# One of four exponential patterns made by an accumulating DMA, in two of three batches

## The chip, the core and the metric

The kernel runs on one core of one Trainium2 chip. The metric is device time in microseconds (us) of that core. The kernel before has a median of 757.29 us in three runs (756.96 to 757.34).

In what follows TensorE (PE in the profile) multiplies matrices, ScalarE (ACT) evaluates functions, VectorE (DVE) and GpSimd (POOL) do elementwise work, and SyncE (SP) issues most DMAs. SBUF is the on-chip memory, PSUM the accumulator memory that TensorE writes, in eight banks of 512 columns.

## The reference

Two attention blocks read the same input x (2048 tokens, 512 features, 32 heads of 16) and are mixed by a gate per token.

```python
x = A_x
g = _sigmoid((x * gate_w).sum(-1, keepdims=True))
# block A: softmax attention
qkv = (x @ wqkv).reshape(B, S, 3, H, Dh)            # q, k, v of 32 heads
scores = jnp.einsum("bhqd,bhkd->bhqk", q, k) * (Dh ** -0.5)
o = jnp.einsum("bhqk,bhkd->bhqd", softmax(scores), v)
a = o.transpose(...).reshape(B, S, D) @ wo
# block B: linear attention with a softmax feature map
phi = concat[softmax(p @ w_phi), softmax(-(p @ w_phi))]   # for q and for k
kv, z = sum_s phi_k v, sum_s phi_k
b = ((phi_q kv) / (phi_q z + 1e-6)).reshape(B, S, D) @ wo
return g * a + (1 - g) * b
```

The exponentials of block A are by far the most work: 32 heads x 2048 x 2048 scores.

## The kernel before

**Tiles.** Scores are kept transposed: keys on the partitions, queries along the columns. A tile (unit) is 128 keys by 512 queries of one head. Four heads make a pack of four tiles, in the four row strips of TensorE; 16 packs, one for each block of 128 keys, make a group of 64 tiles that sums into one PSUM bank; there are 32 groups, so 2048 tiles. A tile goes one of two ways.

**ScalarE's way** (`_qk`, L1040; `_exp`, L1088; `_pv`, L1147). TensorE writes the scores of two tiles into a ring of four PSUM banks, ScalarE takes both in one exponential of 1024 columns into `ET`, a ring of 22 tiles in SBUF (`NSLOT`), and TensorE multiplies by the values V and adds into the group's bank.

**VectorE's way** (`_vector_batch`). `NUMS` says how many tiles of each group go this way, 504 in all. They are handled in batches of four. For each tile TensorE writes scores into a spare bank, and VectorE forms from them, with one multiply and add written as a 16-bit integer (`v_bits`, L946), the bit pattern of a bf16 number that approximates the exponential. One such pattern is coarse, so four are used, with 0, 31, 64 and 95 added to the integer; TensorE multiplies the first two by V and the others by `V2`, which is V times 0.703125, and sums all four. VectorE makes the other three for a whole batch of four tiles (2048 columns) in two additions (`v_step`, L971): the first 2048 columns plus 31 gives the second pattern, then both, 4096 columns, plus 64 give the third and fourth.

```python
src, dst = (va[:, 0, 0:n], va[:, 1, 0:n]) if k == 1 else (va[:, :, 0:n], vs[:, :, 0:n])
```

**Block B and the projections.** They are woven in between: GpSimd does the masks for `qT` (L803), part of the tree sums (L1339), reciprocals (L1392 to L1398), ratio products (L1382), the scaled values V2 (L844) and the normalisation product into T (L1185). SP issues DMAs: four-way copies (T to T, L1191) and DMA transposes that bring normalised outputs (`back`, L1195), feature maps (`phit`, L1451) and block B's outputs (`ontb`, L1509) into the layout for the next product, and the stores (L1653).

**The order.** All instructions of all engines are put in order at build time by a planner (`Plan`). `op` records each operation with its cost, priority and dependences; `order` repeatedly takes, over all engines, the operation that can start earliest by the planned costs, then by priority. `port` keeps GpSimd's operations and VectorE's wide SBUF operations apart in that plan. `shift` adds a pseudo-random offset from `SEEDS` to priorities. On TensorE the planner inserts products with a block of zeros (L1154) where the engine would be little used. On the chip each engine then runs its list strictly in order and waits on semaphores (`emit`, `_waits`).

Of the kernel before, what the change touches and what calls it, by code (L numbers as in the profile page):

```python
# [39 lines left out]
class Op:  # L40
    def __init__(self, eng, fn, cost, name, prio, rel, kind, lat):
        self.eng, self.fn, self.cost, self.name = eng, fn, cost, name
        self.prio, self.rel, self.kind, self.lat = prio, rel, kind, lat
        self.deps = []
        self.users = []
        self.left = 0
        self.need = False
        self.acquire = None
        self.release = None
        self.also = None  # L50
        self.twin = None
# [11 lines left out]
        self.group = None  # L63


class Plan:
# [11 lines left out]
    def __init__(self):  # L78
        self.ops = []
        self.now = -1  # L80
        self.free_banks = []
        self.keep = None
        self.open = None
        self.pad = None
        self.mode = None
        self.strip = [0.0] * 4
        self.n_qk, self.qks, self.exps = 0, (), ()
        self.n_acc = 0
        self.half = None
        self.todo = {}  # L90

# [18 lines left out]
    def op(self, eng, fn, cost, reads=(), writes=(), deps=(), name="", prio=0.0, rel=-99, kind="full",  # L110
# [23 lines left out]
        o.port = eng == "POOL" or eng == "DVE" and name in self.PORT  # L134
# [5 lines left out]
    SEEDS = (3340, 7601, 0, 849, 2310, 7659, 5600, 4117, 3297, 4434, 5571, 2308, 3491, 696, 0, 2037, 1043, 4583, 3197, 9690, 0, 1465, 7801, 8165, 7230, 6142, 5708, 481, 3824, 4801, 1237, 3959, 2876, 7231)  # L140

    def shift(self):
        count = {}
        for o in self.ops:
            k = count[o.name] = count.get(o.name, 0) + 1
            s = self.SEEDS[min(max(int(o.prio // 16), 0), 33)] if o.prio >= 0 else 0
            if s:
                h = sum(map(ord, o.name)) * 7919 + k * 104729 + s * 65537
                h = (h ^ h >> 13) * 2654435761 & 0xFFFFFFFF
                o.prio += (s % 3 + 1) * (((h ^ h >> 16) & 1023) / 511.5 - 1)  # L150
# [64 lines left out]
    def order(self):  # L215
        avail = {e: [] for e in self.ENGS}
        for o in self.ops:
            o.left = len(o.deps)
            for d in o.deps:
                d.users.append(o)  # L220
# [9 lines left out]
        while left:  # L230
            best = None
# [94 lines left out]
    def emit(self, nc, ctx):  # L326
# [6 lines left out]
        count = dict.fromkeys(self.ENGS, 0)  # L333
        for e, q in self.queues.items():
            for o in q:
                if o.name.startswith("dma"):
                    o.sem = (ctx.enter_context(nc.semaphore(o.name)), 16 * len(o.fn) if isinstance(o.fn, list) else 16)
# [70 lines left out]
class _Kernel:  # L408
    NRING = 4
    GROUPS = (2, 2)  # L410
    NSLOT = 22
# [4 lines left out]
    NA, NST, LEAD = 2, 2, 7  # L416
# [21 lines left out]
    ALONE, EARLY = 12, 10  # L438
    PVP = 10
# [18 lines left out]
    def build(self):  # L458
        with ExitStack() as ctx:
# [10 lines left out]
            p.shift()  # L470
# [4 lines left out]
    def _memory(self, ctx):  # L475
# [67 lines left out]
        tiles = [sb(f"vs{k}", [P, 2, self.PACK, QCH], U16) for k in range(self.NST + self.NA)]  # L543
        self.vs, self.va = tiles[:self.NST], tiles[self.NST:]
# [15 lines left out]
    def dma(self, eng, name, fn, cost=0.5, writes=(), reads=(), prio=0.0, rel=-99, lat=2.2, deps=()):  # L560
        return self.plan.op(eng, fn, cost, name="dma_" + name, writes=writes, reads=reads, prio=prio, rel=rel,
                            lat=lat, deps=deps)

# [322 lines left out]
    NUMS = (6, 10, 16, 14, 14, 16, 16, 19, 13, 19, 17, 12, 17, 11, 19, 19, 14, 20, 12, 16, 19, 13, 17, 16, 15, 20, 12, 20, 17, 21, 21, 13)  # L886

    def _plan_vector(self):
# [13 lines left out]
        self.hooks = {}  # L902
# [17 lines left out]
    def _vector_batch(self, number, units, due):  # L920
# [10 lines left out]
        for j, u in enumerate(units):  # L931
# [16 lines left out]
            if j < 2 * pairs and j % 2:  # L948
# [4 lines left out]
                def two(e, j=j, jobs=twin[j // 2]):  # L953
                    lo, hi = sorted(x.bank for x in jobs)
                    return bits(e, va[:, 0, j - 1:j + 1, :], self.ps[:, lo:hi + 1:hi - lo, :])
                parts.append(op("DVE", two, self.c_dve(1024), deps=[first[0], m] + war, name="v_bits", prio=first[2],
                                release=first[1], also=job))
            else:
                parts.append(op("DVE", lambda e, j=j, job=job: bits(e, va[:, 0, j, :], self._bank(job)),
# [4 lines left out]
        slot = self.n_step % self.NST  # L964
        self.n_step += 1
        vs, b_vs, b_vb = self.vs[slot], self.b_vs[slot], self.b_vb[number % self.NA]
        for k in range(4):
            tile, buf = (vs if k > 1 else va)[:, k % 2], b_vs if k > 1 else b_vb if k else b_va
            if k in (1, 2):
                src, dst = (va[:, 0, 0:n], va[:, 1, 0:n]) if k == 1 else (va[:, :, 0:n], vs[:, :, 0:n])  # L970
                o = op("DVE", lambda e, k=k, src=src, dst=dst: e.tensor_scalar(dst, src, float(STEPS[k - 1]), None,  # L971
                                                                               op0=ALU.add),
                       0.16 + k * n * QCH * 0.00026, reads=[b_va] + [b_vb] * (k - 1), writes=[buf], name="v_step",
                       prio=units[0] / 4 - 4)
                o.urgent = units[0] // 4 - self.AHEAD + 2
            v, bufs = (self.V, self.b_V) if k < 2 else (self.V2, self.b_V2)
            for g in sorted({u // (4 * NT) for u in units}):
# [8 lines left out]
                x = op("PE", run, 0.23, reads=[buf], deps=list(found.values()), name="pvx", prio=units[0] / 4 - 2,  # L986
# [6 lines left out]
    def _attention(self):  # L993
        plan, NT, NQC = self.plan, self.NT, self.NQC
        NU = 4 * self.NPACK
        self.exps, self.qks, self.pvs = [], [], []
        self._plan_vector()
# [8 lines left out]
        self.b_va, self.b_vb = [Buf() for _ in range(self.NA)], [Buf() for _ in range(self.NA)]  # L1006
        self.b_vs = [Buf() for _ in range(self.NST)]
        self.n_step = 0
# [9 lines left out]
        self.bank2 = [0, 0]  # L1018
# [60 lines left out]
    def _exp(self, a, b, half=None):  # L1079
# [11 lines left out]
        if a >= len(self.mine) - NR:  # L1091
            o.on_commit = lambda o: plan.free_banks.extend((x % NR, plan._seen(o, "PE"), [o]) for x in range(a, b))
# [70 lines left out]
    def _norm(self, qc, src, side, last, dst, b_dst, due, job, alone=False):  # L1163
# [25 lines left out]
        if side == 1 and not alone and self.P_BACK:  # L1189
# [4 lines left out]
            self.dma("SP", f"mix{due}", parts, cost=11.0, reads=[b_T2], writes=[self.b_T3], prio=due, lat=1.5)  # L1194
            self.dma("SP", f"back{due}", lambda e: e.dma_start(dst.rearrange("p (b t) -> p b t", b=4),  # L1195
                                                               self.T3[:].rearrange("p b f -> p (b f)"), transpose=True),
                     cost=1.3, reads=[self.b_T3], writes=[b_dst], prio=due, lat=1.7)
# [251 lines left out]
    def _b_phit(self, tt, slot, k, due):  # L1449
        op = self.plan.op  # L1450
        self.dma("SP", f"phit{self.n_phit}", lambda e: e.dma_start(  # L1451
            self.phiT[:, :, tt * TOK:tt * TOK + TOK], self.bq[:, slot, k], transpose=True), cost=1.35,
            reads=[self.b_bq[slot]], writes=[self.b_phiT[tt]], prio=due, lat=2.3)
# [53 lines left out]
    def _b_ontb(self, t, due):  # L1507
        tt, slot = t % 4, t % 2
        self.dma("SP", f"ontb{t}", lambda e: e.dma_start(  # L1509
            self.onTB[:, :, tt * TOK:tt * TOK + TOK], self.onB[:, slot, :], transpose=True), cost=1.25,  # L1510
            reads=[self.b_onB[slot]], writes=[self.b_onTB[tt]], prio=due + 1, lat=1.6)
# [84 lines left out]
    def _out(self, qc):  # L1596
        op, NT, NQC = self.plan.op, self.NT, self.NQC
        for tt in range(4):
# [23 lines left out]
            if final and ring:  # L1622
                job.bank = (self.bank2[1] + tt - 4 + self.RINGOUT) % self.NRING
            for x in first:
# [28 lines left out]
            s = self.dma("ACT" if final and tt % 2 else "SP", f"out{t}", lambda e, t=t: e.dma_start(  # L1653
                self.out2d[t * TOK:(t + 1) * TOK, :], self._out_tile(t)), cost=0.36, reads=[b_outt], prio=due)
# [44 lines left out]
```

## Time and profile before

| what | value |
|---|---|
| median of three runs | 757.29 us (756.96 to 757.34) |
| profiled execution: span from first to last instruction | 755.8 us |
| profiled execution: own time beside the span | not listed apart; the runs lie 1.5 us above the span |
| busy ACT / DVE / PE / POOL | 741.1 / 719.9 / 744.3 / 228.6 us |
| ScalarE's exponentials (L1088) | 774 |
| VectorE's bit steps (L946) and additions (L971) | 504 and 252 |
| granted TensorE clock | 1.000 |

The busy times are unions of intervals. Neighbouring instructions on one engine overlap, so a mean duration is longer than the distance from one start to the next. TensorE's busy time contains products that are pipelined and the products with zeros, so it does not say that TensorE is full. The chain of the profile goes back from the last instruction through whatever released each step.

### The profile page before, as it was taken

The page shows a single profiled execution, that of the slowest core. Times are in us where ns is not written, and L with a number is a line of the kernel's source. Part 1 is how long each engine was busy: PE and PEld are TensorE (multiplying, and loading weights), DVE is VectorE, ACT ScalarE, POOL GpSimd, SP SyncE. Part 2 cuts the span into 40 slices and gives each one's busy share as a digit, 9 for nine tenths or more (in the row PEclk, how much of TensorE's full clock was granted, in tenths as well). Part 3 has the DMA queues.
Part 4 walks back from the last instruction along what each step waited for, and adds up shares of the span by engine and source line. Part 5 has one row for each costly group of instructions (what it writes and reads, how often), then busy time and mean ns, then how long its engine had stood idle before and what let it go on. Part 6 is the DMA issues. An engine that isn't in the chain of part 4 may idle for free.

```text
span 755.8 us, 17204 instructions
## 1 busy us (share of the span) xinstructions
PE 744.3 (98%) x7246; PEld 219.7 (29%) x7246; DVE 719.9 (95%) x1128; ACT 741.1 (98%) x796; POOL 228.6 (30%) x317
## 2 busy tenths in 40 slices
PE   8999999999999999999999999999999999999998
PEld 3323222323332222222232323222232222223222
DVE  4788999999999999999999999999999999999997
ACT  6999999999999999999999999999999999999996
POOL 2213206241534334234407051431615051260010
PEclk9999999999999999999999999999999999999999
DMA  9610000001001000000200312112022103111010
GB/s 220 144 24 6 9 8 6 12 2 15 2 2 15 1 8 10 6 11 3 42 15 19 40 24 48 30 34 39 8 47 33 29 23 44 22 30 28 2 15 29
DMA packets 89181, 20.79 MB, mean 28 GB/s; under 512 B 83472, under 2 KB 88592, under 8 KB 89104
## 3 DMA queue, kind: packets, MB, share of 16 engines
q1 hardware_dynamic: 87232, 18.92, 13.8%
q8 instruction: 56, 0.92, 0.5%
q10 hardware_dynamic: 1872, 0.79, 0.4%
q14 instruction: 21, 0.17, 0.1%
HBM read 4.21 MB, written 2.10 MB: 8 GB/s over the span
## 4 chain that ended last, share of the span: by engine, by line
ACT 69%; PE 18%; DVE 11%; DMA 1%; issue 0%
ACT ET L1088 67%; PE ps L1147 6%; PE ps L1040 6%; DVE vs L946 4%; PE ps L711 4%; DVE vs L971 3%; ACT bq L1335 3%; PE ps L1154 1%; DMA xT<-in_A_x_dram 1%; DVE bq L1332 1%; DVE onB L1500 1%; DVE T L1168 0%; DVE rinvB L1483 0%; DVE btree L1329 0%; DVE btree L1327 0%
## 5 line engine op out<-in xcount | busy, mean ns | idle before, releaser
L1088 ACT ACTIVATE ET<-ps 128x1024 bf16<-128x1024 f32 (+1 forms) x774 | 713.4, 1158 | 1.9 <-PE ps L1040 1.5
L946 DVE TENSOR_SCALAR vs<-ps 128x512 uint16<-128x512 f32 x504 | 323.5, 678 | 12.0 <-PE ps L1040 10.1
L1040 PE MATMUL ps<-qT,kT 32*128 32x512 bf16 (+1 forms) x2052 | 307.3, 384 | 4.1 <-ACT ET L1088 2.0
L971 DVE TENSOR_SCALAR vs<-vs 128x2048 uint16<-128x2048 uint16 (+1 forms) x252 | 241.8, 973 | 1.3 <-PE ps L1147 0.5
L1147 PE MATMUL ps<-vs,V 128*32 128x512 bf16 x2016 | 216.9, 384 | 1.1 <-DVE vs L971 0.7
L1147 PE MATMUL ps<-ET,V 128*32 128x512 bf16 x1544 | 193.8, 387 | 0.4 <-DVE vs L946 0.2
L1040 PEld LDWEIGHTS ps<-qT,kT 32*128 32x128 bf16 x2052 | 76.4, 91 | 300.4 <-ACT ET L1088 287.5
L1339 POOL TENSOR_TENSOR btree<-btree 128x512 f16<-128x512 f16 (+1 forms) x32 | 35.7, 1117 | 208.0 <-DVE btree L1337 207.0
L1147 PEld LDWEIGHTS ps<-ET,V 128*32 128x32 bf16 x1544 | 48.6, 94 | 81.3 <-issue 72.2
L1147 PEld LDWEIGHTS ps<-vs,V 128*32 128x32 bf16 x2016 | 50.1, 95 | 49.9 <-issue 28.0
L711 PE MATMUL ps<-WB,xT 128*128 128x512 bf16 x192 | 58.6, 384 | 0.0
L1154 PE MATMUL ps<-kT,zero 128*32 128x512 bf16 x604 | 58.4, 385 | 0.0
L1324 POOL TENSOR_SCALAR bq<-bq 128x1024 bf16<-128x1024 bf16 x16 | 20.2, 1262 | 105.8 <-DVE bq L1306 64.9
L803 POOL TENSOR_SCALAR qT<-qtmp,mask 128x512 bf16<-128x512 bf16 x30 | 26.7, 897 | 55.6 <-DVE qtmp L798 51.0
L711 PE MATMUL ps<-xT,WA 128*128 128x512 bf16 x120 | 37.1, 384 | 0.3 <-DVE onB L1500 0.3
L1185 POOL TENSOR_TENSOR T<-T,rinv 128x512 bf16<-128x512 f32 x15 | 19.6, 1305 | 55.1 <-DVE rinv L1183 54.9
L1335 ACT ACTIVATE bq<-bq 128x2048 bf16<-128x2048 bf16 x16 | 32.8, 2047 | 0.0
L1168 DVE STREAM_TRANSPOSE T<-ps 128x512 f32<-128x512 f32 x32 | 22.6, 706 | 4.5 <-PE ps L1147 4.4
L1306 DVE CAST bq<-ps 128x512 bf16<-128x512 f32 x32 | 21.6, 679 | 0.7 <-PE ps L711 0.6
L844 POOL TENSOR_SCALAR V<-V 128x544 bf16<-128x544 bf16 x16 | 10.7, 670 | 36.0 <-DVE V L837 35.7
L711 PEld LDWEIGHTS ps<-WB,xT 128*128 128x128 bf16 x192 | 13.1, 97 | 24.8 <-issue 20.5
L1332 DVE TENSOR_TENSOR bq<-bq,btree 128x2048 bf16<-128x2048 bf16 x16 | 19.8, 1240 | 0.0
(91 smaller groups left out, 420.9 us busy)
## 6 DMA issues: line engine op xcount, KB each, us to landing
T<-T SPq DMA_DIRECT2D x240, 8.0 KB, 1.8
WB<-in_B_wqkv_dram SPq DMA_DIRECT2D x1, 1536.0 KB, 8.6
out_dram<-WB SPq DMA_DIRECT2D x12, 128.0 KB, 1.7
WA<-in_A_wqkv_dram SPq DMA_DIRECT2D x2, 384.0 KB, 5.3
WoB<-in_B_wo_dram SPq DMA_DIRECT2D x1, 512.0 KB, 3.9
WoA<-in_A_wo_dram SPq DMA_DIRECT2D x1, 512.0 KB, 4.8
WA<-in_A_wqkv_dram ACTq DMA_DIRECT2D x2, 128.0 KB, 3.3
WA<-in_A_wqkv_dram ACTq DMA_DIRECT2D x1, 256.0 KB, 4.9
```

Source lines behind the costliest of these rows:

```text
L711: return e.matmul(out, lhs, rhs, start=start, stop=stop)
L803: x = self.plan.op("POOL", lambda e, side=side: e.tensor_scalar(self.qT[:, s0 + side, :], tmp, self.mask[:, side:side + 1], 0.0, op0=ALU.m ...
L946: bits = lambda e, to, src: e.tensor_scalar(to, src, SCALE * LOG2E * 128.0, float(ORIGIN), op0=ALU.mult, op1=ALU.add)
L971: o = op("DVE", lambda e, k=k, src=src, dst=dst: e.tensor_scalar(dst, src, float(STEPS[k - 1]), None, op0=ALU.add), 0.16 + k * n * QCH * 0 ...
L1040: return e.matmul(out[:, cols], self.kT[32 * i:32 * i + 32, cp, kt * TOK:(kt + 1) * TOK], self.qT[32 * i:32 * i + 32, s, cols], start=True ...
L1088: o = plan.op("ACT", lambda e: e.activation(self.ET[:, a % NS:a % NS + n, cols], self.ps[:, a % NR:a % NR + n, cols], ACT.Exp, scale=SCALE ...
L1147: ins = e.matmul(self._bank(ot)[32 * i:32 * i + 32, :], v[:, v0:v0 + 32], tile, start=(kt == 0), stop=(kt == self.NT - 1), tile_position=( ...
L1154: ins = e.matmul(self._bank(ot)[32 * i:32 * i + 32, :], self.zero[:], self.kT[:, 0, 0:QCH], start=False, stop=False, tile_position=(0, 32 ...
L1168: t1 = op("DVE", lambda e: e.transpose(T1[:, side].rearrange("p b s -> p (b s)"), src()), 0.735, deps=last, writes=[b_T1[side]], name="n_t ...
L1332: + [("b_sub", two(2048), lambda e: e.tensor_tensor(x, x, spread(tree[:, :, 0]), ALU.subtract))],
L1335: op("ACT", lambda e: e.activation(flat, flat, ACT.Exp), 1.789, reads=[b], writes=[b], name="b_exp", prio=due + 1)
L1339: + [("b_sum", two(128 * n), lambda e, n=n: e.tensor_tensor(half[:, :, 0:n], half[:, :, 0:n], half[:, :, n:2 * n], ALU.add), (n <= self.P_ ...
```

## The change

In two of three batches (`KINDS = 'DDV'`; not in the first four nor the last two, `PLAIN`) the pattern with 64 added is no longer made by VectorE. After TensorE has used the first pattern, GpSimd issues a DMA that adds a constant tile `steps`, filled with 64, to the tile in place (`accum_op=ALU.add`), and TensorE reads the same tile again as the third pattern. In the other batches VectorE makes the same addition in place. The patterns with 31 and 95 are made by VectorE from the first, each by an addition of 2048 columns, so no addition of 4096 columns is left. The buffers change with it: five tiles `va` that hold a first pattern, two pairs `vb`, the constant tile, and `ET` with 16 tiles instead of 22.

`NUMS` gives VectorE 548 tiles instead of 504 (60 instead of 46 in the first four groups). The planner now has a model of the time for which the DMA engines are moving an addition (`moves`, `chan`): copies and transposes that are issued meanwhile are planned to land later. A DMA issue on GpSimd does not count for `port`. The offsets of `shift` are drawn anew every eight steps of the plan from 64 new seeds, so that the whole order differs.

```diff
-        o.port = eng == "POOL" or eng == "DVE" and name in self.PORT
+        o.port = eng == "POOL" and not name.startswith("dma") or eng == "DVE" and name in self.PORT
...
+    EVERY = 8
+    FIRST, LANDED, BEHIND = 1.45, 1.3, 1.5
...
+                if o.moves > 0:
+                    self.chan = max(t + self.FIRST, self.chan) + o.moves
+                    o.lat = self.chan + self.LANDED - o.end
+                    for x in self.small:
+                        if x.end + x.lat > t + self.FIRST:
+                            x.lat = max(x.lat, self.chan + self.BEHIND - x.end)
+                elif o.moves <= -100:
+                    o.lat = max(o.lat, self.chan + self.BEHIND - o.end)
+                    self.small = [x for x in self.small if x.end + x.lat > t] + [o]
+                elif o.moves < 0:
+                    o.lat += min(-o.moves, max(0.0, self.chan - o.end))
...
-    NSLOT = 22
+    NSLOT = 16
...
-    NA, NST, LEAD = 2, 2, 7
+    NA, NB, LEAD = 5, 2, 7
...
+    C_ADD, MOVES, ADD_AT, PVD = 0.9, 2.8, -1, 0
+    KINDS, PLAIN = 'DDV', (4, 2)
...
-    NUMS = (6, 10, 16, 14, 14, 16, 16, 19, 13, 19, 17, 12, 17, 11, 19, 19, 14, 20, 12, 16, 19, 13, 17, 16, 15, 20, 12, 20, 17, 21, 21, 13)
+    NUMS = (8, 16, 20, 16, 16, 20, 17, 15, 18, 18, 18, 18, 15, 18, 17, 15, 18, 17, 16, 16, 18, 20, 17, 21, 16, 16, 16, 18, 16, 21, 20, 17)
...
-        for k in range(4):
-            tile, buf = (vs if k > 1 else va)[:, k % 2], b_vs if k > 1 else b_vb if k else b_va
-            if k in (1, 2):
-                src, dst = (va[:, 0, 0:n], va[:, 1, 0:n]) if k == 1 else (va[:, :, 0:n], vs[:, :, 0:n])
-                o = op("DVE", lambda e, k=k, src=src, dst=dst: e.tensor_scalar(dst, src, float(STEPS[k - 1]), None,
-                                                                               op0=ALU.add),
...
+        tiles = [(va, b_va), (vb[:, 0], b_v1), last, (va, b_va)]
+
+        def make(dst, by, reads, writes, prio):
+            o = op("DVE", lambda e: e.tensor_scalar(dst[:, 0:n], va[:, 0:n], float(by), None, op0=ALU.add),
+                   0.16 + n * QCH * 0.00026, reads=reads, writes=writes, name="v_step", prio=prio)
...
+        def add(k, tile, buf):
+            o = self.dma("POOL", f"add{number}_{k}", lambda e: e.dma_start(tile[:, 0:n], self.steps[:, 0:n], accum_op=ALU.add),
+                         cost=self.C_ADD, reads=[self.b_steps], writes=[buf], prio=units[0] / 4 + self.ADD_AT)
...
+        make(vb[:, 0], STEPS[0], [b_va], [b_v1], units[0] / 4 - 4)
+        if kind != "E":
+            make(vb[:, 1], sum(STEPS), [b_va], [b_v3], units[0] / 4 - 4)
+        for k in (0, 1, 2, 3) if kind != "E" else (0, 1, 3, 2):
+            tile, buf = tiles[k]
+            if k == 3 and kind == "V":
+                make(va, STEPS[1], [], [b_va], units[0] / 4 - 1)
+            elif k == 3 or k == 2 and kind == "E":
+                add(k, tile, buf)
```

More of the change, by code (lines that the diff above doesn't have):

```diff
@@ L216, in order @@
         avail = {e: [] for e in self.ENGS}
+        count = {}
         for o in self.ops:
+            k = count[o.name] = count.get(o.name, 0) + 1
+            o.base, o.code = o.prio, sum(map(ord, o.name)) * 7919 + k * 104729
             o.left = len(o.deps)
@@ L562, in dma, with moving @@
                             lat=lat, deps=deps)
+    def moving(self, o, moves, late=0.0):
+        o.moves = -moves
+        o.lat += late
+        return o
     def _loads(self):
```

89 lines of the change are left out of this document (53 added, 36 removed).

## The prediction

> **What bounds the kernel now.** I read the head of the page first, then its chain, then the groups by shape, the stretches of 25 us, and last the chain and the timeline piece by piece.
>
> ```profile
> span 755.8 us, 17204 instructions
> PE 744.3 (98%) x7246; PEld 219.7 (29%) x7246; DVE 719.9 (95%) x1128; ACT 741.1 (98%) x796; POOL 228.6 (30%) x317
> ACT 69%; PE 18%; DVE 11%; DMA 1%; issue 0%
> ```
>
> ScalarE is busy for 741.1 of 755.8 us and carries 69% of the chain, so its work sets the end. VectorE is close behind with 719.9. The three runs have a median of 757.29 us, 1.5 us above this span; I sum against the span and add 1.5 at the end. A difference of 0.2% (1.5 us) is about what a measurement of this kernel can tell from none.
>
> The stretches say where each engine has room (columns: PE, PEld, DVE, ACT, POOL busy):
>
> ```profile
> 0.00:25.00 25.00, 22.57 (x140) 8.79 (x143) 14.29 (x26) 17.92 (x23) 6.27 (x18) 1.00 1.05 229
> 25.00:50.00 25.00, 25.00 (x244) 8.08 (x237) 18.45 (x27) 25.00 (x29) 6.07 (x8) 1.00 0.17 47
> 50.00:75.00 25.00, 25.00 (x206) 8.17 (x204) 22.78 (x38) 25.00 (x27) 5.79 (x11) 1.00 0.10 22
> 75.00:100.00 25.00, 24.99 (x234) 6.90 (x231) 23.69 (x41) 25.00 (x29) 5.12 (x7) 1.00 0.08 12
> ...
> 550.00:575.00 25.00, 24.22 (x278) 7.78 (x277) 24.67 (x39) 25.00 (x27) 9.82 (x15) 1.00 0.17 32
> ...
> 725.00:750.00 25.00, 24.93 (x259) 7.19 (x258) 23.32 (x37) 22.42 (x25) 0.00 (x0) 1.00 0.07 10
> 750.00:775.00 25.00, 2.79 (x13) 1.07 (x11) 2.41 (x4) 1.08 (x2) 0.00 (x0) 0.98 0.06 21
> ```
>
> ScalarE's 14.7 us of idle time lie almost wholly at the start (7.1) and the end (2.6 and 4.7). VectorE's 35.9 split otherwise: 10.7, 6.6, 2.2 and 1.3 in the first 100 us (20.8), 1.7 and 3.4 in the last two rows (5.1), and so only 10.0 in the 625 us between. There both engines are nearly full, and a change pays only if it takes work from both.
>
> **What one operation costs.** A group's mean is a duration, and neighbours overlap, so I count from start to start. In the chain in order of time (start, length, what), and in the timeline of VectorE:
>
> ```profile
> 560.88 49.50 ACT ET L1088 x54
> ```
>
> ```profile
> 373.97 1.21 DVE L971 TENSOR_SCALAR vs<-vs 128x4096 uint16<-128x4096 uint16 x1
> 375.10 0.68 DVE L946 TENSOR_SCALAR vs<-ps 128x512 uint16<-128x512 f32 x1
> 375.70 0.24 DVE L1476 SCALAR_TENSOR_TENSOR rinvB<-ps,ghB,eps 128x32 f32<-128x32 f32 x1
> 375.85 0.68 DVE L971 TENSOR_SCALAR vs<-vs 128x2048 uint16<-128x2048 uint16 x1
> 376.45 0.24 DVE L1476 SCALAR_TENSOR_TENSOR rinvB<-ps,ghB,eps 128x32 f32<-128x32 f32 x1
> ```
>
> One exponential of two tiles costs ScalarE 49.50/54 = 0.917 us. On VectorE the next instruction starts 0.60 us after a 512-column bit step (375.10 to 375.70), 0.60 after a 2048-column step (375.85 to 376.45) and 1.13 after a 4096-column one (373.97 to 375.10).
>
> **ScalarE.** 548 tiles instead of 504 go to VectorE, so 44/2 = 22 exponentials fall away: 22 x 0.917 = 20.2 us. Busy 741.1 becomes 720.9; with its idle time unchanged the span is 735.6, the time 737.1. That is the floor on this engine.
>
> **VectorE.** Groups by shape of before (count, then busy and mean):
>
> ```profile
> L946 DVE TENSOR_SCALAR vs<-ps 128x512 uint16<-128x512 f32 x504 | 323.5, 678 | 12.0 <-PE ps L1040 10.1
> L971 DVE TENSOR_SCALAR vs<-vs 128x4096 uint16<-128x4096 uint16 x126 | 154.9, 1233 | 0.8 <-PE ps L1147 0.5
> L971 DVE TENSOR_SCALAR vs<-vs 128x2048 uint16<-128x2048 uint16 x126 | 89.1, 713 | 0.5
> ```
>
> In the issue order of the changed kernel stand 548 bit steps, no 4096-column step, and 324 of 2048 columns: two for each of 137 batches and a third for the 50 that VectorE completes itself. The other 87 batches have a DMA issue on POOL instead. Added: 44 x 0.60 = 26.4 and 324 x 0.60 = 194.4; removed: 126 x (0.60 + 1.13) = 218.0. The net is +2.8 us, so VectorE needs 722.7. The eleven extra batches eat what the DMA saves; the gain is ScalarE's alone, provided VectorE finds room in a shorter span: at 735.6 its idle time must fall from 35.9 to 12.9.
>
> Where is that room? One tile cost 0.60 + 1.73/4 = 1.03 us; it now costs 0.90 in a DMA batch, 1.05 in a VectorE batch, 0.95 in the two-to-one mix. The 32 groups of 64 tiles take 23.6 us each, so the first four are the first 94 us; there the table gives VectorE 60 tiles instead of 46. The first sixteen are plain: 16 x 1.05 + 44 x 0.95 - 46 x 1.03 = +11.2 us, against 10.1 idle after the first 25 us and 10.7 in them, which is mostly waiting for the loads. ScalarE would allow 7 x 0.917 = 6.4 there; I take half, 3.2. In the other 28 groups (488 tiles for 458) VectorE saves 458 x 1.03 - 488 x 0.95 = 8.1 us, and ScalarE 15 x 0.917 = 13.8. If VectorE keeps its 10.0 us of idle time, this part gains 8.1; if it gives up 5.7 of them, 13.8. I take 13.8, because the largest part of that idle is the row's 10.1 us of bit steps that wait for scores, a wait that the slower ScalarE leaves room for, not a need. So 757.3 - 3.2 - 13.8 = 740.3, between 749.2 (8.1, and nothing early) and 737.1.
>
> **The DMA and its wait.** Each of the 87 adds a constant tile to 128x2048 two-byte elements, 512 KB, in place in SBUF. No such transfer is in the trace. Nearest rows:
>
> ```profile
> T<-T SPq DMA_DIRECT2D x240, 8.0 KB, 1.8
> WoB<-in_B_wo_dram SPq DMA_DIRECT2D x1, 512.0 KB, 3.9
> WoA<-in_A_wo_dram SPq DMA_DIRECT2D x1, 512.0 KB, 4.8
> ```
>
> A plain load of the same size lands 3.9 us after its issue, against 1.8 for a small copy, so its moving takes about 2.1. An addition in place has two tiles to read; with the moving doubled I estimate 6.0 us (ends: 3.9, and 4.8 plus 3.0 = 7.8 with the slower load doubled likewise). TensorE takes its instructions in order, so when it reaches the values of this pattern too early, scores and then ScalarE stop behind it. The issue order fixes how early: between TensorE's last read of the tile as bits and its read after the addition lie 4 score pairs that wait for ScalarE in 1 batch, 5 in 3, 6 in 6, 7 in 17, 8 in 14, more in 46. At 0.917 us each that is 3.7, 4.6, 5.5, 6.4 and 7.3 us. About 0.9 us of a stall is hidden, since the four score banks hold one activation ahead. At 6.0 us the cost is (2.3 - 0.9) + 3 x (1.4 - 0.9) = 2.9 us; at 3.9 nothing. I take 2.9: 743.2, rounded to **743**.
>
> **What I cost at nothing.**
>
> ```profile
> L1147 PE MATMUL ps<-vs,V 128*32 128x512 bf16 x2016 | 216.9, 384 | 1.1 <-DVE vs L971 0.7 <-DVE vs L946 0.4
> L1154 PE MATMUL ps<-kT,zero 128*32 128x512 bf16 x604 | 58.4, 385 | 0.0
> POOL btree L1339 <- DVE btree L1337: 207.0, 16, 25.6
> DVE btree L1327 <- POOL bq L1324: 1.2, 1, 1.2
> SPq L1191 <- POOL T L1185: 235.4, 12, 41.3
> L1382 POOL TENSOR_TENSOR bq<-bq,brec 128x512 bf16<-128x512 bf16 x16 | 18.1, 1133 | 1.1
> ```
>
> TensorE gets 4 x 44 - 44 = 132 more value products (0.108 us of busy time each, +14.2) and 300 instead of 604 products with zeros (0.097 each, -29.4): no load. POOL gets 87 issues; bounded by its 1133 ns row, 99 us on an engine with 527 us idle. Of these, 52 wait for TensorE and 57 for VectorE, and behind them queue POOL's masks for qT, its tree sums, reciprocals and T products. POOL now waits 207.0 us for the tree alone, VectorE waits 1.2 us for POOL: that slack is the cover; without it a late tree delays VectorE by up to an issue (1.1 us) in each of 16 pairs, 18 us. The transposing copies on SP share the 16 engines with 87 x 2.1 to 4.2 = 183 to 365 us of moving. SP itself now waits 235.4 us for T, so a copy later by one addition is mostly not missed; uncovered, 32 such copies of branch B by 4.2 us would be 134. The tile ring of 16 makes an exponential wait for values 8 activations (7.3 us) back instead of 11: products queued behind a late pattern hold it, which the stall above already counts. The new order of everything can move single waits either way; ScalarE, at 25.00 in nearly every stretch, has none to gain in the middle.
>
> **Rivals.** *VectorE stays the bound with its idle time* (35.9 us in all, nothing early filled): 722.7 + 35.9 + 1.5 = 760.1; with the early room used and the middle's idle time kept, 749.2. For it: 98% busy in the middle. Against: its waits there are for scores.
>
> *The additions land late, slower than before.* The place is the in-order read on TensorE; at 8 us from last read to landing the cost is 3.4 + 3 x 2.5 + 6 x 1.6 + 17 x 0.7 = 32 us, the time 740.3 + 32 = 772. It decides from about 7.4 us (16 to 17 us lost, no gain left). For it: doubling the slower load plus issue gives that; against: 46 batches wait over 7.3 us anyway.
>
> *VectorE's wide steps and POOL's descriptor writing block each other.* Today's row: a step alone takes 0.68, the mean of 126 is 713 ns, so POOL's 228.6 us cost 0.03 us a step, with an order that keeps them apart. The new order does not keep the issues apart from the steps: 99 us of POOL time are 13% of 740 us, 43 of 324 steps would meet one and wait half of it, 0.57: 24 us, of which the idle time covers 10. In the other direction two steps in a row hold an issue for 1.2 us: 7.2 instead of 6.0, 12.6 us by the sum above. Together 740.3 + 14 + 12.6 = 767. This mechanism is the rule of the Trainium skill, page "SBUF — State Buffer", section "SBUF: two separate sides": while VectorE runs a two-port mode, GpSimd cannot write the descriptors of its DMAs, and whichever starts first keeps the port. The trace bears it out weakly, by the 0.03 us; no DMA from POOL is in it.
>
> That the change does nothing is excluded by the issue order: the 87 additions are there.
>
> **How the numbers follow.** Forecast (737 to 749): 0.65. VectorE bound: 0.12, of it 0.07 faster, 0.03 same, 0.02 slower. Landing late: 0.14. Port: 0.09. Faster 0.72, same 0.03, slower 0.25. The range runs from 735 (two us less idle at start and end than now) to 767, where half of the two slow cases lie above: left out are some 0.13 above and 0.03 below. The forecast's own range is 737 to 749.
>
> **What would show it.** Right: ScalarE busy near 721 with about 15 to 20 idle; about 722 on VectorE; TensorE's waits for the additions below 5 us in all; landing under 7 us. Wrong: a large TensorE wait on the additions (landing), 2048-column steps with a mean well above 713 ns (port), or ScalarE idle spread over the middle with VectorE at 99% (VectorE bound).

## The result and the profile after

The median goes from 757.46 us to 755.05 us (20 runs each); the ratio is 0.9968, 95% interval 0.9958 to 0.9978. That is 0.3% faster, 12 us short of the forecast of 743. The head of the page of the changed kernel (its profiled execution took 757.03 us; PEld is TensorE's loading of weights, and a q behind an engine's name stands for its sequencer):

```profile
span 754.9 us, 17015 instructions
PE 722.3 (96%) x7011; PEld 217.4 (29%) x7078; DVE 726.1 (96%) x1244; ACT 725.2 (96%) x774; POOL 284.4 (38%) x405
PE 34%; DVE 30%; ACT 27%; DMA 7%; issue 2%; DVEq 0%
```

ScalarE lost 15.9 us of work (20.2 were forecast), but the span shrank by 0.9: ScalarE now idles for 29.7 us instead of 14.7, and its share of the chain fell from 69% to 27%. The groups that answer to those shown of before, and the landing of the new transfers:

```profile
L1141 ACT ACTIVATE ET<-ps 128x1024 bf16<-128x1024 f32 (+1 forms) x752 | 696.9, 1118 | 17.5 <-PE ps L1093 12.8
L988 DVE TENSOR_SCALAR va<-ps 128x512 uint16<-128x512 f32 x548 | 353.9, 678 | 7.4 <-PE ps L1093 5.9
L1011 DVE TENSOR_SCALAR vb<-va 128x2048 uint16<-128x2048 uint16 x274 | 194.2, 726 | 0.5 <-PE ps L1201 0.5
L1016 POOL DMA_DIRECT2D va<-steps x87 | 82.5, 952 | 274.2 <-PE ps L1201 142.9
L1011 DVE TENSOR_SCALAR va<-va 128x2048 uint16<-128x2048 uint16 x50 | 36.7, 733 | 1.6 <-PE ps L1201 1.6
va<-steps POOLq DMA_DIRECT2D x87, 512.0 KB, 5.0
```

The additions land in 5.0 us. ScalarE's new idle time is 12.8 us of waiting for scores, and VectorE waits for scores too (5.9), although it is at 96%. Among the waits, those that name an addition are small:

```profile
ACT ET L1141 <- PE ps L1093: 12.8, 20, 2.4
...
PEld ps L1201 <- DMA va<-steps: 7.1, 10, 1.5
DVE va L988 <- PE ps L1093: 5.9, 18, 0.6
```

Ten waits, none over 1.5 us: no single late transfer, although their sum of 7.1 us is above the 5 that the prediction gave as a sign of being right. Stretches show where the time goes (columns: PE, PEld, DVE, ACT, POOL busy, granted clock, DMA share, GB/s); the first row is the kernel before, the others the changed one:

```profile
350.00:425.00 75.00, 73.97 (x768) 21.05 (x766) 74.44 (x113) 74.83 (x81) 27.57 (x37) 1.00 0.15 28
...
325.00:350.00 25.00, 24.44 (x243) 7.12 (x246) 24.83 (x43) 25.00 (x27) 10.79 (x18) 1.00 0.23 44
350.00:375.00 25.00, 23.75 (x227) 6.71 (x226) 24.08 (x41) 22.19 (x24) 11.82 (x17) 0.93 0.54 96
375.00:400.00 25.00, 23.18 (x228) 7.37 (x227) 24.96 (x43) 23.91 (x26) 8.35 (x11) 1.00 0.23 43
400.00:425.00 25.00, 23.23 (x231) 6.46 (x229) 23.87 (x40) 22.49 (x24) 12.95 (x18) 0.93 0.54 96
```

From 325 to 350 us ScalarE is full; in the next 75 it loses 6.4 us, where before it lost 0.2. The granted clock, 1.00 there before, falls to 0.93 in two stretches, and in these two every engine has idle time. In the first of the two, the timeline (start, length, engine, line; brackets give the idle time before an instruction and what ended it):

```profile
363.95 0.69 DVE L1011 TENSOR_SCALAR va<-va 128x2048 uint16<-128x2048 uint16 x1
...
364.34 0.86 POOL L1016 DMA_DIRECT2D va<-steps  x1 [5.68 <-PE ps L1201]
...
364.55 2.39 DVE L1011 TENSOR_SCALAR vb<-va 128x2048 uint16<-128x2048 uint16 x1
...
364.91 2.56 POOL L1394 TENSOR_TENSOR btree<-btree 128x512 f16<-128x512 f16 x2
...
366.86 0.68 DVE L988 TENSOR_SCALAR va<-ps 128x512 uint16<-128x512 f32 x1
...
367.60 0.39 PE L1093 MATMUL ps<-qT,kT 32*128 32x512 bf16 x1 [1.10 <-DVE va L988]
...
367.92 0.97 PE L1201 MATMUL ps<-vb,V 128*32 128x512 bf16 x4
```

Read it downwards. GpSimd issues an addition at 364.34. Its next operation, a tree sum (L1394), starts 0.57 us after that. In between, at 364.55, VectorE starts a 2048-column step, which takes 2.39 us instead of 0.69. VectorE's next bit step therefore starts at 366.86, about 1.7 us late, TensorE stands for 1.10 us until it has freed a bank, and afterwards TensorE's own products run at a lower clock (four products start to end in 0.97 us, where such a group took 0.60 earlier in the same kernel, at 359.16). ScalarE, fed by those products, is busy for only 1.02 of the 3.40 us from 368.0 on, in which the granted clock is 0.50:

```profile
368.00:371.40 3.40, 3.40 (x26) 0.71 (x26) 2.98 (x6) 1.02 (x1) 1.50 (x3) 0.50 0.40 66
```

The same happens at 411 us behind another issue, with a negation (L1379); the held step is the second of the two in the first row, from 411.26, and takes 2.36 us:

```profile
410.66 2.96 DVE L1011 TENSOR_SCALAR vb<-va 128x2048 uint16<-128x2048 uint16 x2
...
411.09 0.88 POOL L1016 DMA_DIRECT2D va<-steps  x1 [0.65 <-PE ps L1201]
...
411.74 1.33 POOL L1379 TENSOR_SCALAR bq<-bq 128x1024 bf16<-128x1024 bf16 x1
...
414.27 0.39 PE L1093 MATMUL ps<-qT,kT 32*128 32x512 bf16 x1 [1.22 <-DVE va L988]
```

And at 395 us, where the next operation behind the issue starts with the step:

```profile
395.12 0.86 POOL L1016 DMA_DIRECT2D va<-steps  x1 [4.58 <-PE ps L1201]
395.67 2.04 DVE L1011 TENSOR_SCALAR vb<-va 128x2048 uint16<-128x2048 uint16 x1
395.69 2.55 POOL L1394 TENSOR_TENSOR btree<-btree 128x512 f16<-128x512 f16 x2
...
397.77 0.40 PE L1201 MATMUL ps<-vb,V 128*32 128x512 bf16 x4 [1.24 <-DVE vb L1011]
```

Here TensorE stands for 1.24 us, and the clock stays at 1.00. The clock is the smaller part of the loss of 12 us: the five of the 20 runs whose granted clock was 1.000 throughout took 752.90 to 755.63 us, with a median of 753.77. In the three places the first operation of GpSimd behind the issue ends at 366.38, 397.15 and 413.07 us (the two tree sums of a row counted singly), and the step ends 0.55 or 0.56 us after it.

That makes a theory. The planner keeps GpSimd's operations apart from VectorE's wide steps (`port`), but it plans an issue at 0.9 us (`C_ADD`), and on the chip GpSimd's next operation, where nothing else holds it (18 of the 87), starts after 0.56 to 0.65. It then arrives at the moment for which VectorE's step is planned, and the step is held until that operation ends. The rivals: the bytes of the additions are late or in the way; the issue itself blocks VectorE; or VectorE is simply full.

### The profile page after: what moved, and what is told of

Same layout as the page of the kernel before. It is cut to its first block, busy times and chain, and to the rows that moved or that the text cites. A ratio compares the mean times of both kernels' runs of the same rounds, so it can differ in the third digit from the quotient of the medians.

```text
span 754.9 us, 17015 instructions
## 1 busy us (share of the span) xinstructions
PE 722.3 (96%) x7011; PEld 217.4 (29%) x7078; DVE 726.1 (96%) x1244; ACT 725.2 (96%) x774; POOL 284.4 (38%) x405
## 4 chain that ended last, share of the span: by engine, by line
PE 34%; DVE 30%; ACT 27%; DMA 7%; issue 2%; DVEq 0%
ACT ET L1141 26%; DVE va L988 14%; PE ps L1201 13%; PE ps L1093 11%; DVE vb L1011 7%; DMA va<-steps 7%; PE ps L753 6%; PE ps L869 2%; ACT bq L1390 1%; PE ps L1208 1%; DVE va L1011 1%; DVE T L1222 1%; DVE onB L1555 1%; DVE bq L1361 1%; DVE bq L1387 1%
## 5 line engine op out<-in xcount | busy, mean ns | idle before, releaser
L1141 ACT ACTIVATE ET<-ps 128x1024 bf16<-128x1024 f32 (+1 forms) x752 | 696.9, 1118 | 17.5 <-PE ps L1093 12.8
L988 DVE TENSOR_SCALAR va<-ps 128x512 uint16<-128x512 f32 x548 | 353.9, 678 | 7.4 <-PE ps L1093 5.9
L1011 DVE TENSOR_SCALAR vb<-va 128x2048 uint16<-128x2048 uint16 x274 | 194.2, 726 | 0.5 <-PE ps L1201 0.5
L1016 POOL DMA_DIRECT2D va<-steps x87 | 82.5, 952 | 274.2 <-PE ps L1201 142.9
L1201 PE MATMUL ps<-vb,V 128*32 128x512 bf16 x1096 | 133.4, 385 | 1.8 <-DVE vb L1011 1.7
L1201 PE MATMUL ps<-va,V 128*32 128x512 bf16 x1096 | 131.2, 385 | 4.0 <-DMA va<-steps 3.8
L1394 POOL TENSOR_TENSOR btree<-btree 128x512 f16<-128x512 f16 (+1 forms) x32 | 36.7, 1146 | 23.3 <-DVE btree L1392 22.5
L1379 POOL TENSOR_SCALAR bq<-bq 128x1024 bf16<-128x1024 bf16 x16 | 18.1, 1133 | 55.7 <-DVE bq L1361 35.9
L1201 PEld LDWEIGHTS ps<-va,V 128*32 128x32 bf16 x1096 | 31.4, 95 | 26.3 <-issue 11.7
L1201 PEld LDWEIGHTS ps<-vb,V 128*32 128x32 bf16 x1096 | 31.5, 95 | 24.8 <-issue 12.5
L1011 DVE TENSOR_SCALAR va<-va 128x2048 uint16<-128x2048 uint16 x50 | 36.7, 733 | 1.6 <-PE ps L1201 1.6
L1208 PE MATMUL ps<-kT,zero 128*32 128x512 bf16 x300 | 31.3, 393 | 0.0
```

Source lines behind the costliest of these rows:

```text
L988: bits = lambda e, to, src: e.tensor_scalar(to, src, SCALE * LOG2E * 128.0, float(ORIGIN), op0=ALU.mult, op1=ALU.add)
L1011: o = op("DVE", lambda e: e.tensor_scalar(dst[:, 0:n], va[:, 0:n], float(by), None, op0=ALU.add), 0.16 + n * QCH * 0.00026, reads=reads, w ...
L1016: o = self.dma("POOL", f"add{number}_{k}", lambda e: e.dma_start(tile[:, 0:n], self.steps[:, 0:n], accum_op=ALU.add), cost=self.C_ADD, rea ...
L1141: o = plan.op("ACT", lambda e: e.activation(self.ET[:, a % NS:a % NS + n, cols], self.ps[:, a % NR:a % NR + n, cols], ACT.Exp, scale=SCALE ...
L1201: ins = e.matmul(self._bank(ot)[32 * i:32 * i + 32, :], v[:, v0:v0 + 32], tile, start=(kt == 0), stop=(kt == self.NT - 1), tile_position=( ...
L1208: ins = e.matmul(self._bank(ot)[32 * i:32 * i + 32, :], self.zero[:], self.kT[:, 0, 0:QCH], start=False, stop=False, tile_position=(0, 32 ...
```

## The experiments

All keep every queue's order of the changed kernel, and change only what single instructions do or wait for. Medians, and ratios to the kernel before on the same chip:

| kernel | median us | ratio, 95% interval |
|---|---|---|
| the change | 755.05 | 0.9968 (0.9958 to 0.9978) |
| no issues | 746.66 | 0.9854 (0.9837 to 0.987) |
| issues of 16 columns | 753.54 | 0.9947 (0.9933 to 0.996) |
| short GpSimd operations | 743.95 | 0.9818 (0.9804 to 0.9833) |
| 269 waits on GpSimd | 758.34 | 1.0008 (0.9987 to 1.003) |
| 49 waits behind an issue | 757.12 | 0.9976 (0.995 to 1.0002) |
| 269 waits, additions after copies | 765.99 | 1.0113 (1.0092 to 1.0135) |
| 49 waits, additions after copies | 760.18 | 1.0037 (1.0024 to 1.005) |
| 49 waits, one addition later | 747.00 | 0.9865 (0.9849 to 0.9882) |
| 49 waits, issues of 16 columns | 743.80 | 0.9817 (0.9802 to 0.9831) |
| 269 waits, one addition later | 754.33 | 0.9951 (0.9925 to 0.9976) |

**No issues at all.** The 87 DMAs are left out (the third pattern is wrong in their batches).

```diff
-  lambda e: e.dma_start(tile[:, 0:n], self.steps[:, 0:n], accum_op=ALU.add),
+  [],
```

> The changed kernel with all engines in the same order, but without the 87 DMA issues (the third pattern of those batches stays without its 64; POOL still waits where an issue stood). Theory port: in the changed kernel POOL's wide operation that follows an issue starts while a 2048-column step of VectorE is about to run, and holds it for 1.4 to 1.7 us; PE then stands still and its clock halves. Without issues POOL's next operation starts earlier still, so some collisions may stay: 741 to 750 us, the mean of the 2048-column steps below 715 ns. Theory landing (TensorE waits for the additions): 741 to 744 us, since that wait is gone. Theory VectorE full (no room in any case): 752 to 755 us.

746.66 us, so 8.4 of the missing 12 us hang on the DMAs in some way, by their bytes or by their issue.

**Issues that move next to nothing.** The DMA adds 16 of 2048 columns.

```diff
-  lambda e: e.dma_start(tile[:, 0:n], self.steps[:, 0:n], accum_op=ALU.add),
+  lambda e: e.dma_start(tile[:, 0:1, 0:16], self.steps[:, 0:1, 0:16], accum_op=ALU.add),
```

> The changed kernel in the same order, with the 87 DMAs cut to 16 columns each (the third pattern gets its 64 in those columns alone). The issues stay on POOL, the moving of 512 KB goes. Theory port: no gain, 752 to 756 us, the steps' excess as it was (mean 726 ns). Theory landing: 741 to 746 us. Theory VectorE full: 752 to 755 us.

753.54 us: in this order the bytes are 1.5 us of it, and the rest hangs on the issue. The stretch from 350 to 425 us loses nearly the same without them:

```profile
350.00:425.00 75.00, 70.33 (x687) 20.32 (x686) 73.28 (x124) 69.20 (x72) 34.22 (x46) 0.95 0.15 16
```

ScalarE busy for 69.20 of 75 us at a clock of 0.95, with the DMA share at 0.15: late or colliding transfers are out as the main cause.

**Short operations on GpSimd.** Tree sums, negations and ratio products work on an eighth or a sixteenth of their elements (block B's output is incomplete); all 87 additions are whole. The edit of the tree sums:

```diff
-  e.tensor_tensor(half[:, :, 0:n], half[:, :, 0:n], half[:, :, n:2 * n], ALU.add)
+  e.tensor_tensor(half[:, 0:2, 0:n], half[:, 0:2, 0:n], half[:, 0:2, n:2 * n], ALU.add)
```

> The changed kernel in the same order and with its DMAs, but POOL's tree sums, negations and ratio products on block B cut to a sixteenth or an eighth of their size (so block B's result is left incomplete): an operation behind an issue then holds VectorE for 0.2 us instead of 1.4. Theory port: 741 to 747 us, steps' mean 690 to 705 ns, TensorE's clock at 1.0. Theory landing: 753 to 756 us. Theory VectorE full: 752 to 755 us.

743.95 us. Its page:

```profile
span 742.0 us, 17082 instructions
...
L1011 DVE TENSOR_SCALAR vb<-va 128x2048 uint16<-128x2048 uint16 x274 | 184.4, 691 | 0.5 <-PE ps L1201 0.4
L1016 POOL DMA_DIRECT2D va<-steps x87 | 83.9, 967 | 297.3 <-PE ps L1201 141.6
```

The issues are there, as long as before, but the steps' mean falls from 726 to 691 ns and the forecast's time appears. So the issue by itself does not block VectorE, and VectorE is not full: what the steps meet is GpSimd's computing operations. The trace of the changed kernel says the same when its 324 steps are counted singly: 58 overlap an issue and nothing else on GpSimd, with a median of 684 ns and a greatest of 724, and the 186 that overlap nothing there have 684 and 696.

**Every GpSimd operation waits for the step planned before it.** A pass behind the planner adds, for 269 of GpSimd's 314 computing operations, a wait for the last wide VectorE operation planned to end before it, if that end lies less than 3 us back.

```diff
+    wide = [o for o in queues["DVE"] if o.port]
+    for x, o in zip([None] + queues["POOL"], queues["POOL"]):
+        if not o.port or behind and not (x is not None and x.name.startswith("dma")):
+            continue
+        first = [d for d in wide if d.end <= o.start + 0.001]
+        if first and first[-1].end > o.start - reach:
+            o.deps.append(first[-1])
```

> The changed kernel in the same order, complete, with a wait added: each operation of POOL that uses the port waits for the last wide operation of VectorE that the plan puts ahead of it (if it ends less than 3 us earlier). VectorE waits for nothing new. Theory port: the collisions behind an issue go, 742 to 749 us. If a late POOL operation then meets the next step instead, 750 to 756 us with the long steps in other places. Theory landing: 753 to 757 us. Theory VectorE full: 752 to 755 us.

758.34 us: a miss in time. Most of it lies at one place. In the stretch from 350 to 425 us ScalarE is busy for 74.75 us, so that loss is gone, but from 600 to 640:

```profile
350.00:425.00 75.00, 73.63 (x753) 22.39 (x751) 74.83 (x135) 74.75 (x79) 37.31 (x56) 1.00 0.51 89
600.00:640.00 40.00, 32.39 (x274) 7.88 (x272) 28.92 (x51) 29.42 (x32) 7.25 (x8) 0.87 0.74 75
```

10.6 us of ScalarE's time go there, at a DMA share of 0.74 and only 75 GB/s.

**Waits behind an issue alone.** The same pass with `behind=True`: 49 operations.

> Order of every queue as after the change; the only edit is that the 49 of GpSimd's 314 computing operations that stand right behind an addition's issue also wait for the last 2048-column step of VectorE that the plan puts before them. If the loss is the step that a GpSimd operation behind an issue overtakes and holds (theory), the jumps at 364, 398 and 411 to 419 us go, and the time falls to 745 (743 to 750), with the steps' mean back from 733 ns to about 700. If the loss is the moving of the additions or VectorE being full (rival), those waits change nothing or add to it: 755 to 758.

757.12 us (two of twelve runs at 748.18 and 752.63): again the first loss is gone (ScalarE is busy for 74.93 of the 75 us) and another has come. The DMAs issued from 597 to 620 us, and GpSimd's and SP's part of the timeline:

```profile
va<-steps POOLq DMA_DIRECT2D x2, 512.0 KB, 15.4
out_dram<-WB SPq DMA_DIRECT2D x2, 128.0 KB, 14.8
phiT<-bq SPq DMA_TRANSPOSE x2, 15.6
```

```profile
601.75 0.88 POOL L1016 DMA_DIRECT2D va<-steps  x1
...
601.83 4.83 SPq L1506 DMA_TRANSPOSE phiT<-bq  x2
```

An addition issued 0.08 us ahead of two transposing copies: all transfers of that moment land after about 15 us, where the median of all additions is 5.0. TensorE waits for the addition, up to 7.8 us at once. In the kernel with 269 waits the same two were issued 0.09 us apart and landed in 13 to 15 us; in the changed kernel the addition came 0.8 us after the first copy, and the copies landed in 5.5 us. Nearness alone is not enough, though. In this same run an addition issued at 542.06 us stands 0.02 us ahead of two transposing copies of WT (542.08 and 543.39), and nothing crawls, though its issue took 1.33 us instead of 0.88. The second of these copies lands in 5.4 us; for the addition and the first copy the profile has

```profile
va<-steps POOLq DMA_DIRECT2D x1, 512.0 KB, 6.0
...
WT<-onB SPq DMA_TRANSPOSE x1, 3.3
```

What sets the place at 601 us apart from this one was not tested. The next runs test whether the addition costs the time at that place.

**Additions wait for transposing copies.** Any addition planned from 1 us before to 2.5 us after a copy of phiT (five of the 87) waits for it to land; with the 269 waits and with the 49.

```diff
+    turned = [o for o in queues["SP"] if o.name.startswith("dma_phit")]
...
+        if apart and o.moves > 0:
+            o.deps += [d for d in turned if d.start - 1 < o.start < d.start + apart]
```

> The kernel with every one of GpSimd's operations made to wait for the step planned before it lost 11.5 us at one place, where an addition was issued at 602.23 us and two transposing copies of phiT at 602.32, and all of them landed after about 14 us. Here an addition planned within 1 us before or 2.5 us after such a copy waits for the copy to land, and nothing else differs from that kernel. If the coincidence of the two kinds of transfer is the cause (theory), the time falls from 758.3 to 747 (745 to 750). If the place was lost for another reason, such as VectorE late by the added waits (rival), it stays at 758, or the waiting of GpSimd's queue for the copies makes it worse (760).

> Both edits at once: the waits behind an issue alone (49 operations), and additions kept from the transposing copies of phiT. By the theory of the overtaken steps 744 to 748, no more than 2 us from the run with the 49 waits alone, since the additions and copies do not coincide in that one unless it slips otherwise. If the additions' landing is what costs (rival), this one gains over that by more than 2 us, or stays at 755.

Both worse, 765.99 and 760.18 us, neither as the theory had it. The waits of the first:

```profile
PEld ps L1201 <- DMA va<-steps: 16.9, 11, 4.7
```

TensorE's waits for additions are 16.9 us in all, where with the 269 waits alone they were 13.9. The crawling is gone (from 597 to 620 us additions land in 4.8 us and the copies of phiT in 4.3), but from 425 to 600 us these waits rose from 3.7 to 12.0 us, and ScalarE is busy for 161.51 us instead of 173.18: additions that are held back come too late. So this remedy neither confirms the cause nor refutes it.

**One addition later.** Only the addition at that place also waits for an operation of VectorE, the first that by the plan ends 1.0 us or more after the issue's planned start. It was then issued at 602.87 us, 1.75 us behind the first copy (601.12).

```diff
+    turned = [o for o in queues["SP"] if o.name.startswith("dma_phit")][::2]
...
+        if later and o.moves > 0 and any(abs(d.start - o.start) < 0.3 for d in turned):
+            o.deps += [d for d in queues["DVE"] if o.start + later <= d.end][:1]
```

> The kernel with the 49 waits behind an issue ran without a loss up to 606 us (its exponentials at the plan's times less a constant 3.5 to 2.4 us) and then lost 11 us at one place: an addition was issued at 601.73 us, 0.1 us ahead of two transposing copies of phiT, and all transfers there landed after about 15 us. Here that one addition also waits for VectorE's next operation, which puts its issue about 1.2 us later, behind the start of the copies; nothing else differs. If the coincidence is the cause (theory): 746 (744 to 749), and the landing at that place is back at 5 to 6 us. If additions beside copies crawl whatever their order (rival): 757 again. Delay of an addition that has no slack (second rival): 749 to 752, with TensorE waiting on va for 2 to 4 us there.

747.00 us (745.57 to 748.33), 1.35% below before and the fastest kernel here that leaves nothing out. At the place, and for the head, the groups and the steps' spread (nanoseconds: least, median, greatest):

```profile
va<-steps POOLq DMA_DIRECT2D x4, 512.0 KB, 6.0
out_dram<-WB SPq DMA_DIRECT2D x2, 128.0 KB, 4.8
phiT<-bq SPq DMA_TRANSPOSE x2, 4.9
```

```profile
span 743.8 us, 17025 instructions
PE 716.9 (96%) x7011; PEld 216.9 (29%) x7078; DVE 717.4 (96%) x1244; ACT 723.5 (97%) x774; POOL 281.7 (38%) x405
ACT 49%; PE 29%; DVE 15%; DMA 5%; issue 1%; POOL 0%; DVEq 0%
L1011 DVE TENSOR_SCALAR vb<-va 128x2048 uint16<-128x2048 uint16 x274 | 187.9, 703 | 0.5 <-PE ps L1201 0.3
```

```profile
L1011 DVE TENSOR_SCALAR vb<-va x274: 618/682/1644, 21.1 to 727.7; 128x2048 uint16<-128x2048 uint16 x137
```

(The changed kernel's row has 617/684/2387.) Landing is normal again at the place, so the addition at that moment cost the 10 us. Steps longer than 1 us fell from 13 to 5, and the time that all steps together take beyond 684 ns each from 15.4 to 7.8 us. Of the 13, seven stood behind an issue with GpSimd's next operation, and six met an operation that no issue preceded; of the 5 left, one stands behind an issue. And at the place of the first loss:

```profile
363.62 1.02 POOL L1016 DMA_DIRECT2D va<-steps  x1 [5.68 <-PE ps L1201]
...
363.83 0.69 DVE L1011 TENSOR_SCALAR vb<-va 128x2048 uint16<-128x2048 uint16 x1
...
364.65 1.92 POOL L1394 TENSOR_TENSOR btree<-btree 128x512 f16<-128x512 f16 x2
```

The step, 0.21 us behind the same issue as in the changed kernel, takes 0.69 us: only the tree sum has moved behind it. Two sums take 1.92 us instead of 2.56 as well. The issue grew from 0.86 to 1.02 us, and that is all that the issue and the step do to each other here.

**The 49 waits with issues of 16 columns.**

> The kernel with the 49 waits behind an issue, its additions cut to 16 of 2048 columns, so that their issues stay and their bytes go (one of four patterns is then wrong). If the loss at 602 us is the addition's bytes beside the copies (theory): the copies land there in 3 to 6 us and the time is 745 (743 to 748), equal to what the kernel gives once the two are kept apart. If it is the issue or the queue that holds the copies (rival): 755 to 758.

743.80 us. With the issue 0.08 us ahead of the copies as in the run that lost there (600.95 and 601.03), the copies land in 4.9 us: it is the addition's bytes, not its issue, that crawl with them. The bytes' whole price, once the rest is mended, is 747.00 - 743.80 = 3.2 us. And this is the cleanest measure of the waits: between the two kernels with issues of 16 columns nothing differs but the 49 waits, and the time falls from 753.54 to 743.80, by 9.7 us.

**The 269 waits, one addition later.**

> All of GpSimd's operations wait for the step planned before them, and the one addition is issued 1.2 us later as in the run beside it. By the theory 747 (745 to 750): 758.3 less the 11.5 us of the one place, and no better than with 49 waits, because the operations behind an issue are the ones that hurt. If the other 220 waits are worth something of their own (rival): 742 to 744.

754.33 us (748.16 to 758.67), a miss on both sides. From 600 to 640 us:

```profile
600.00:640.00 40.00, 35.07 (x324) 9.42 (x326) 35.05 (x61) 35.40 (x38) 9.79 (x12) 0.96 0.51 77
```

ScalarE is busy for 35.40 us instead of 29.42 with the 269 waits alone, so part of that loss stays; additions there land in 8.7 us, although the first is issued 1.47 us behind the first copy. So a distance from the copies alone does not say how they land. A gain from the other 220 waits does not show; why transfers still drag there I have not separated.

The order being the same in all, the start of the k-th exponential in the traces shows each loss as a jump (us from the start of the span):

| k | the change | 49 waits | 49 waits, one addition later | 49 waits, 16 columns |
|---|---|---|---|---|
| 340 | 336.6 | 336.4 | 335.9 | 336.1 |
| 380 | 378.1 | 374.9 | 374.4 | 374.7 |
| 420 | 420.8 | 413.4 | 412.9 | 413.2 |
| 620 | 617.7 | 608.7 | 608.0 | 607.9 |
| 640 | 637.4 | 637.8 | 627.4 | 626.1 |
| 750 | 744.1 | 743.3 | 732.9 | 731.2 |

Between exponentials 340 and 420 the change loses 7.2 us against the mended kernel, and 3.3 more by the end (these are the profiled executions, 757.03 and 745.57 us, further apart than the medians); the kernel with 49 waits follows it to 620 and then loses 9.7 in 20 exponentials.

## Why the prediction was wrong

**The step that failed** is the line of the sum that has no term for the port: 99 us of issues on GpSimd stood under "What I cost at nothing", with a late tree as their only price, and the port was only a rival with a chance of 0.09. It took most of the missing time. From 755.05 to 747.00 us, with the order at the port held by waits and the one addition moved, is 8.0 us, two thirds of what separates the result from the forecast; the waits alone, with the bytes gone in both kernels, are worth 9.7.

**The rival named the right place and the wrong partner.** It had the steps wait for descriptor writing and issues held for 1.2 us, 767 in all. Measured, an issue that is alone with a step costs the step nothing (a median of 684 ns with and without), and 27 of the 87 issues are 0.16 to 0.46 us longer than 0.86, not 1.2; landing did not suffer, and 767 was too high. What the issue does is to let the operation behind it start about 0.3 us before its planned time, against a step. The three longest such steps, 2.39, 2.36 and 2.04 us, lie in the stretch from 350 to 425 us, where ScalarE loses 6.4 us; the rest of the loss comes in smaller jumps later. The sign "2048-column steps with a mean well above 713 ns" came only weakly, as 726 and 733: a few long steps show in the greatest value, not in the mean. The Trainium skill, page "SBUF — State Buffer", section "SBUF: two separate sides", says that a GpSimd operation and a VectorE operation in a two-port mode exclude each other for the whole of the one that starts first. The runs agree on the exclusion (2.39 against 0.69 us), but the step at 364.55 started before the sum at 364.91 by the trace and was held all the same; which of the two had the port first, no run here shows. The descriptor writing that the section also names was lengthened here by at most 0.46 us.

**The terms that held.** Landing was estimated at 6.0 us and measured 5.0. Its price, 2.9 us in the sum, is 3.2 by the two mended kernels, but that agreement is luck: at 5.0 us the same sum gives 1.3 - 0.9 = 0.4, so the rest of the 3.2 comes by a way that the sum did not have. ScalarE: 720.9 us forecast, 723.5 once mended (725.2 in the change). VectorE: 722.7 forecast, 717.4 once mended; the 726.1 of the change holds the steps' waiting. Early and middle: 740.3 without landing was forecast, 743.80 measured with the bytes gone, 3.5 us off: 1.8 of it ScalarE's busy time (722.7), the rest about its idle time, of which 11.1 us lie in the first 50 instead of 7.1. So the result is 740.3 + 3.5 + 3.2 + 8.0 = 755.0; the last three are each the difference of one time to the next, so they add up by themselves.

**The other rivals.** Late additions do not end the changed kernel: no wait is over 1.5 us. But the bytes beside transposing copies, which the prediction put at nothing because SP has slack, took 10 us at one place in two kernels; in the change the addition happened to come 0.8 us behind the first copy there. VectorE as the bound is refuted: with the waits it does the same work 8 us sooner.

The chances were wrong in the same place. That the gain could go wholly to a port conflict had been worked out, but a new order of GpSimd's queue should have weighed more than 0.09, since `port` no longer counted issues and the planned length of one, 0.9 us, stood in no trace of the kernel before.

## What to carry to other kernels

When an issue of a DMA goes to GpSimd, look at the operation behind it: if a hand-made order keeps that engine and VectorE's wide steps apart by planned times, state the order as a wait, at the few places where it matters (with the one addition moved, 49 waits gave 8.0 us and 269 gave 0.7). Give a step that is late on an engine at 96% its full price, because the wait passes through TensorE to ScalarE. When an added wait gives nothing, look for the next place that is late: one addition issued together with two transposing copies hid the whole gain of the 49 waits, and issuing it 1.75 us behind the first copy brought it back, where a wait for the copies' landing did not.

## What the runs showed of the hardware

- An accumulating DMA of 512 KB within SBUF lands 5.0 us after its issue (median of 87); 6.0 between other transfers at 600 us.
- An issue on GpSimd takes 0.83 to 0.95 us in 60 of 87 cases and 1.02 to 1.32 in the other 27, 25 of which overlap a 2048-column step of VectorE, as do 30 of the 60. Where nothing else holds it, GpSimd's next operation starts 0.56 to 0.65 us after the issue's start.
- Three 2048-column steps of VectorE that began 0.36, 0.48 and 0.02 us before that next operation were held until it had ended: they took 2.39, 2.36 and 2.04 us instead of 0.68. Beside an issue alone a step keeps its 0.68.
- At one place, in two kernels, an addition issued 0.08 to 0.09 us before two DMA transposes made every transfer of that moment land after 13.7 to 15.6 us (medians by kind). Issued 1.75 us after the first of them it left them at 4.9, and with 16 columns instead of 2048 it did so even at 0.08. At another place, 0.02 us before two transposes of another tile, they landed in 3.3 and 5.4 and the addition in 6.0.
- Twice, after TensorE had stood for 1.10 and 1.22 us in the middle of full work, its granted clock was 0.50 for 3.4 us (from 368.0 and from 415.8 us); after a stand of 1.24 us between the two it stayed at 1.00.
